# Linear attention into an MLP: joint tails, a reordered start, a held load and a split copy

## The chip, the cores and the metric

The program runs on one core of one Trainium2 chip. The metric is the device time of one execution in microseconds (us), taken as the median of several runs. The kernel before has a median of 296.78 us over 9 runs, from 296.37 to 297.11.

The engines are named as in the profile: PE is TensorE's matrix multiply and PEld its weight load, DVE is VectorE, ACT is ScalarE, POOL is GpSimd, and SP is SyncE, which only issues DMAs here. Every engine works through its own instructions in order.

## The reference

The inputs q, k and v have 8 batches, 8 heads, 576 positions and 64 features per head. Linear attention feeds an MLP (w_in is 512x2048, w_out is 2048x512, beta has 2048 entries):

```
phi(x) = where(x > 0, x, exp(x) - 1) + 1
kv  = sum over s of phi(k)[s, :, None] * v[s, None, :]      # per batch and head
z   = sum over s of phi(k)[s]
x   = (phi(q) @ kv) / (phi(q) @ z + 1e-6)                   # heads side by side: 4608 x 512
h   = x @ w_in
out = (h * sigmoid(beta * h)) @ w_out                       # float32, 4608 x 512
```

The kernel computes in bf16 with f32 accumulation. The loads of q, k, v and w_in cast from f32 to bf16 on the way, w_out is divided by beta on the chip, and the gate is then one Silu with a scale of beta.

## The kernel before, in words

**Tiles.** A batch has 576 rows: four tiles of 128 (t = 0 to 3) and a tail of 64 (t = 4, `NJ`). The MLP runs on the four full tiles of one batch at a time (512 columns), and once more, as batch `B` = 8, on the tails of all batches, which are gathered in `xT_tail` (8 x 64 columns). Batch 0 is laid out in another way: nine rows j on 64 partitions, with two groups of four heads on the lower and the upper half of the partitions (`nine`, `load_nine`, and the functions that end in 0).

**Stages of a batch n.** Exp on ScalarE (`exp_`), max(x, 0) + 1 on DVE (`relu`) and their minimum (`phi`, which gives phi of the reference). `v_copy` puts v beside a column of ones. `kv_mm` makes kv and z on TensorE: 40 small matmuls, alternating between output rows 0-63 and 64-127. `kv_evac` copies them out of PSUM into the block-diagonal `kv_bd[n % 2]`. phi(q) is transposed on TensorE (`q_trans`, batches 0 and 1) or by one DMA issued from SP (`q_trans_dma`, from batch 2). Then for each tile: `num_mm` (four matmuls of 130 columns), `num_norm` (three DVE instructions: add, reciprocal, multiply) and the transpose of the result into `xT`, by TensorE (`x_trans`, batches 0 to 2, with a copy out of PSUM) or by a DMA from SP (from batch 3, `DMA_T`).

**MLP.** `h_phase` does h for the 16 blocks of 128 of d_ff, each four matmuls and one Silu on ScalarE. `y_phase` (or `y_phase_wide`, four tiles side by side, for batches 0 and 1) multiplies by w_out; each tile of y is copied and stored by SP.

**Order.** It is written out by hand (`manual_schedule`). While batch b is in its MLP, batch n = b + 1 is prepared: a `plan` gives, for an index i, the functions that are issued after group i of an h_phase, or after ff block i (and then after tile i - 12) of `y_phase_wide`, or after every four ff blocks in `y_phase`. From batch 2 on this is one loop (for b in 2 to 8). A function's instructions enter the in-order queues of their engines at that place.

**Buffers.** PSUM: four banks in the pool `mm`, and two double banks in the pool `att`, used in turn by kv_mm, num_mm, the "wide" transposes and the last h blocks of batches 0 and 1. `xqk` has three buffers, `vraw` and `vaug` two each, `q_pT` two.

**Loads.** GpSimd issues the casting loads, in order: batch 0's k, q (j < 4), v (j < 6), v (rest), q (rest), the four pieces of w_in, w_out's first two pieces, batch 1's k and q, and so on. `load_next(b)` issues six DMAs (main part and tail of k, q and v). `load_next(3)` is issued in y_phase_wide(0), `load_next(4)` in h_phase(1), and later ones after an h_phase.

**The start.** To occupy TensorE before data arrive, `warm` multiplies a zeroed tile. Batch 0 then goes through exp0, relu0, phi0, kv_mm0, q_trans0 and num_mm for tiles 0 and 1; the second part of q (j from 4) is worked on between.

**Lines.** Large matmuls are L453 (h) and L505 (y); num_mm is L399, x_trans L433, kv_mm L344, kv_evac L355, q_trans L380, copies out of PSUM L372 (ACT) and L370 (DVE), v_copy L370, exp L229, Silu L445, num_norm L413 to L415, batch 0's loads L131, other loads L72 and L76, w_in L159, silu_table L581, warm L575.

Of the kernel before, what the change touches and what calls it, by code (L numbers as in the profile page):

```python
# [16 lines left out]
def kernel(  # L17
# [99 lines left out]
    def nine(a, spec):  # L117

        names = " ".join(spec)
        flat = a.rearrange("p a b c -> p (a b c)")  # L120
        size = {"h": HH, "j": N9, "d": D}
        n = size["h"] * size["j"] * size["d"]
        return flat[:, 0:n].rearrange(f"p ({names}) -> p {names}", **size)

    q9 = nine(xqk[0][:, 0], "hjd")
    k9 = nine(xqk[0][:, 1], "hjd")
    v9 = nine(vraw[0], "hjd")

    def load_nine(dst, src, h0=0, h1=HH, j0=0, j1=N9):
        for g in range(2):  # L130
            nc.gpsimd.dma_start(  # L131
                out=dst[g * TAIL : (g + 1) * TAIL, h0:h1, j0:j1, :].rearrange(
                    "p h j d -> p h (j d)"
                ),
                in_=src[0, g * HH + h0 : g * HH + h1, :, :]
# [7 lines left out]
    nc.vector.memset(g_sb[0][:, FC - 1, :], 0.0)  # L143
    clear_tail(1)
    nc.vector.memset(vraw[1][TAIL:P, :, NJ, :], 0.0)
    beta_row = consts.tile([FC, P], F32)
    nc.sync.dma_start(out=beta_row, in_=moe_beta.rearrange("(c p) -> c p", p=P))
# [3 lines left out]
    load_nine(k9, k)  # L151
    load_nine(q9, q, j1=4)
    make_identity(nc, identity)
    make_identity(nc, ident16)
    load_nine(v9, v, j1=6)
    load_nine(v9, v, j0=6)
    load_nine(q9, q, j0=4)
# [90 lines left out]
    x0 = {0: q9, 1: k9}  # L248
# [4 lines left out]
    def exp0(a, j0, j1):  # L253
        if j0 == 0:
            st["e0", a] = work9("e", bufs=3)
        nc.scalar.activation(  # L256
            st["e0", a][:, j0:j1].rearrange("p j h d -> p h j d"), x0[a][:, :, j0:j1],
            ACTF.Exp,
        )

    def relu0(a, j0, j1):
        if j0 == 0:
            st["r0", a] = work9("r")
        nc.vector.tensor_scalar(
            st["r0", a][:, j0:j1].rearrange("p j h d -> p h j d"), x0[a][:, :, j0:j1],
# [3 lines left out]
    def phi0(a, j0, j1):  # L269
        nc.vector.tensor_tensor(  # L270
            st["p0"][a][:, j0:j1], st["r0", a][:, j0:j1], st["e0", a][:, j0:j1], ALU.min
        )

    def q_trans0(t, banks, c0):


        for jj in range(2 if t < NJ else 1):
            for a in range(2):
                for g in range(2):
# [4 lines left out]
                        st["p0"][0][gs, 2 * t + jj, 2 * a : 2 * a + 2, :],  # L284
# [4 lines left out]
    def q_out0(t, banks, c0, dve):  # L289
        n = rows(t)  # L290
        src = banks[:, :, c0 : c0 + 2 * P].rearrange("p g (a n) -> p g a n", a=2)
        dst = st[0, "qT"][:, t].rearrange("p (g a) n -> p g a n", g=2)
# [483 lines left out]
```

## Time and profile before

| What | Value |
|---|---|
| median of 9 runs | 296.78 us |
| profiled execution, its own time | 297.11 us |
| its span, first to last instruction | 295.3 us |
| mean granted TensorE clock | 0.993 |
| first h matmul | 17.26 us |
| w_in's first piece, issued / landed | 8.39 / 17.2 us |
| first y matmul on record, batch 0 | 35.17 us |
| first h matmul of batches 1, 2, 3 | 52.82, 85.53, 116.66 us |
| HBM read, written | 36.71 MB, 9.44 MB |

Times are counted from the span's start. A timeline line gives start, duration, engine, line, operation, tiles (out<-in), shape, count, and in brackets the idle time of the engine before it with what ended that wait. "128*64" in a matmul is rows times columns of the weights, "128x130" the moving data. A matmul's duration runs to the end of its pipeline; the distance between starts is what it costs in a stream. A few matmul records are missing from a trace. A "stretch" line gives start:end and length, then each engine's busy time with its instructions, then the granted clock as a share of full speed, the DMA engines' mean busy share, and GB/s, which counts the bytes as written (bf16 where a load casts).

### The profile page before, as it was taken

How to read it: one execution, taken by the hardware profiler on the slowest of the kernel's cores; microseconds unless marked ns; L12 is line 12 of the kernel's file. 1: busy time of each engine (PE TensorE's matmuls, PEld its weight loads, DVE VectorE, ACT ScalarE, POOL GpSimd, SP SyncE). 2: the span in 40 equal slices, each digit the busy share in tenths (PEclk: the TensorE clock that was granted, in tenths of full speed). 3: DMA queues.
4: the chain of work that ended last, by engine and by line, in shares of the span. 5: the costliest groups of instructions: out<-in, count | busy, mean ns of one | idle time of the engine just before them, and what ended most of it. 6: DMA issues, size and time to landing. Idle time of an engine off the chain costs nothing.

```text
span 295.3 us, 4750 instructions
## 1 busy us (share of the span) xinstructions
PE 284.4 (96%) x1891; PEld 145.1 (49%) x1912; DVE 123.5 (42%) x261; ACT 175.3 (59%) x234; POOL 53.4 (18%) x72
## 2 busy tenths in 40 slices
PE   8879999999989999999999999999999999999994
PEld 3467446744555454445444544454445444444444
DVE  5665388504366164616461647154715400110012
ACT  2788795889988780778087907790770077018500
POOL 8924575540003200330023000000000000000000
PEclk9979999999999999999999999999999999999999
DMA  7999999999437993699369955024502400120032
GB/s 106 197 204 343 261 274 190 258 191 189 82 142 97 175 137 110 128 174 153 100 130 158 156 112 124 2 71 115 127 0 72 118 36 0 38 87 19 0 73 71
DMA packets 72310, 37.09 MB, mean 126 GB/s; under 512 B 40912, under 2 KB 66784, under 8 KB 72288
## 3 DMA queue, kind: packets, MB, share of 16 engines
q0 software_dynamic: 38912, 20.45, 47.7%
q1 hardware_dynamic: 33216, 16.20, 22.9%
q8 instruction: 15, 0.25, 0.3%
q10 hardware_dynamic: 160, 0.13, 0.2%
q14 instruction: 7, 0.06, 0.1%
HBM read 36.71 MB, written 9.44 MB: 156 GB/s over the span
## 4 chain that ended last, share of the span: by engine, by line
PE 80%; DMA 11%; ACT 3%; POOL 2%; issue 2%; DVE 0%; POOLq 0%
PE mm L453 37%; PE mm L505 35%; DMA xqk<-in_q_dram 5%; DMA vraw<-in_v_dram 3%; DMA w_in<-in_moe_w_in_dram 3%; PE att L399 3%; PE att L344 2%; POOL xqk L131 1%; PE mm L537 1%; PE att L453 1%; POOL vraw L131 1%; ACT e L229 1%; ACT g L445 1%; PE mm L433 1%; ACT L229 0%
## 5 line engine op out<-in xcount | busy, mean ns | idle before, releaser
L445 ACT ACTIVATE g<-mm,beta_c 128x512 bf16<-128x512 f32 (+2 forms) x156 | 97.3, 633 | 88.8 <-PE mm L453 88.6
L505 PE MATMUL mm<-w_out,g 128*128 128x512 bf16 x541 | 126.7, 379 | 1.2 <-issue 0.3
L453 PE MATMUL mm<-xT,w_in 128*128 128x512 bf16 (+2 forms) x560 | 108.9, 351 | 1.1 <-DMA w_in<-in_moe_w_in_dram 1.1
L453 PEld LDWEIGHTS <-w_in 128*128 128x128 bf16 x656 | 62.5, 99 | 62.1 <-DMA w_in<-in_moe_w_in_dram 1.2
L505 PEld LDWEIGHTS <-g 128*128 128x128 bf16 x560 | 52.9, 98 | 58.3
L515 DVE COPY y_sb<-mm 128x512 f32<-128x512 f32 x27 | 18.7, 691 | 70.6 <-PE mm L505 69.1
L229 ACT ACTIVATE e<-xqk 128x2560 bf16<-128x2560 bf16 x14 | 31.9, 2329 | 0.1
L415 DVE TENSOR_TENSOR xs<-att,rden 128x512 bf16<-128x512 f32 (+1 forms) x40 | 27.6, 690 | 1.4
L242 DVE TENSOR_TENSOR qk_p<-r,e 128x2560 bf16<-128x2560 bf16 x14 | 20.9, 1492 | 13.2 <-ACT e L229 12.4
L72 POOL DMA_DIRECT2D vraw<-in_v_dram x7 | 7.0, 996 | 85.0 <-DVE vaug L370 79.0
L355 DVE CAST kv_bd<-att 64x130 bf16<-64x130 f32 x28 | 8.2, 292 | 32.7 <-PE att L344 32.3
L413 DVE TENSOR_SCALAR den<-att 128x8 f32<-128x8 f32 (+1 forms) x40 | 6.5, 161 | 32.9 <-PE att L399 32.8
L399 PEld LDWEIGHTS <-q_pT 128*128 128x128 bf16 (+1 forms) x160 | 12.0, 102 | 10.1 <-DVE xs L415 2.4
L399 PE MATMUL att<-kv_bd,q_pT 128*128 128x130 bf16 (+1 forms) x160 | 16.2, 226 | 0.7 <-DVE kv_bd L370 0.7
L453 PE MATMUL mm<-xT_tail,w_in 128*128 128x512 bf16 x63 | 13.9, 379 | 0.1
L237 DVE TENSOR_SCALAR r<-xqk 128x2560 bf16<-128x2560 bf16 x14 | 11.4, 817 | 3.9 <-DMA xqk<-in_q_dram 2.4
L575 PE MATMUL mm<-g 128*128 128x512 bf16 x34 | 9.4, 435 | 1.2 <-DVE g L143 1.2
L229 ACT ACT_TABLE_LOAD x7 | 9.0, 1283 | 0.1
L414 DVE RECIPROCAL rden<-den 128x8 f32<-128x8 f32 (+1 forms) x40 | 8.1, 202 | 1.4
L72 POOL DMA_DIRECT2D xqk<-in_k_dram x7 | 6.8, 977 | 5.8 <-DMA w_in<-in_moe_w_in_dram 2.8
L76 POOL DMA_DIRECT2D xqk<-in_k_dram x7 | 7.4, 1062 | 1.6 <-DMA w_in<-in_moe_w_in_dram 1.6
L256 ACT ACTIVATE e<-xqk 128x1280 bf16<-128x1280 bf16 (+1 forms) x4 | 4.4, 1155 | 5.5 <-DMA xqk<-in_k_dram 4.9
(71 smaller groups left out, 140.4 us busy)
## 6 DMA issues: line engine op xcount, KB each, us to landing
out_dram<-y_sb SPq DMA_DIRECT2D x28, 256.0 KB, 2.3
xqk<-in_k_dram POOLq DMA_DIRECT2D x7, 512.0 KB, 10.6
xqk<-in_q_dram POOLq DMA_DIRECT2D x7, 512.0 KB, 11.6
vraw<-in_v_dram POOLq DMA_DIRECT2D x7, 512.0 KB, 11.2
w_in<-in_moe_w_in_dram POOLq DMA_DIRECT2D x4, 512.0 KB, 11.5
g<-in_moe_w_out_dram POOLq DMA_DIRECT2D x4, 512.0 KB, 10.7
out_dram<-y_sb SPq DMA_DIRECT2D x14, 128.0 KB, 5.2
xqk<-in_moe_w_out_dram POOLq DMA_DIRECT2D x2, 512.0 KB, 14.6
```

The lines of the kernel that those rows point to most:

```text
L72: eng.dma_start(out=dst[:, :, 0:NJ, :].rearrange("p h j d -> p h (j d)"), in_=src[b, :, 0:MAIN, :].rearrange("h (p j) d -> p h (j d)", j=NJ),)
L229: nc.scalar.activation(st[b, "e", a][:, h0:h1], xqk[b % NX][:, a, h0:h1], ACTF.Exp)
L237: nc.vector.tensor_scalar(st[b, "r", a][:, h0:h1], xqk[b % NX][:, a, h0:h1], 0.0, 1.0, ALU.max, ALU.add)
L242: nc.vector.tensor_tensor(st[b, "p"][:, a].rearrange("p j (h d) -> p h j d", h=H)[:, h0:h1], st[b, "r", a][:, h0:h1], st[b, "e", a][:, h0: ...
L355: nc.vector.tensor_copy(kv_bd[b % 2][i][gs, :, g, :], st[b, "kvp"][gs, 2 * i : 2 * i + 2, :])
L399: nc.tensor.matmul(nps[:n, p // 2, c0 : c0 + 2 * (D + 1)], st[b, "qT"][:, t, p, :n], kv_bd[b % 2][p // 2][:, p % 2], start=True, stop=True ...
L415: nc.vector.tensor_mul(xs[:n], nv[:, :, :, 0:D], rden[:n, :, :, None].to_broadcast([n, 2, 4, D]))
L445: nc.scalar.activation(g_sb[b % 2][:, ff, c0:c1], hp[:, c0:c1], ACTF.Silu, scale=beta_c[:, ff : ff + 1],)
L453: nc.tensor.matmul(hp[:, c0:c1], w_in_sb[ff // 4][:, kc, (ff % 4) * P : (ff % 4 + 1) * P], x[:, t0:t1, kc, :] if b < B else x[:, kc, c0:c1 ...
L505: nc.tensor.matmul(yp, g_sb[b % 2][:, ff, t * P : (t + 1) * P], w_out_sb[ff // 4][:, ff % 4, :], start=(ff == 0), stop=(ff == FC - 1),)
L515: nc.vector.tensor_copy(y_sb, yp)
L575: nc.tensor.matmul(st["warm"], g_sb[0][:, FC - 1, 0:P], g_sb[0][:, FC - 1, :], start=True, stop=True, skip_group_check=True,)
```

## The change

**Joint tails.** The tails of batches b - 1 and b (b = 1, 3, 5, 7) are normalized together. num_mm(b, NJ) does eight matmuls, batch b - 1 into rows 0-63 and batch b into rows 64-127; num_norm works on 128 rows, and one DMA transpose from SP puts the result into 128 columns of xT_tail, for all batches. The even batches' tail steps and the x_trans of tails go.

**Start.** The last four of batch 0's nine k rows per partition (`KF` = 5) are loaded as f32 by SP into `k_last`, a part of g_sb[1], instead of by GpSimd with a cast; exp and relu read it there. beta's load is issued by ScalarE. v is split at 5 instead of 6. There are 25 warm matmuls instead of 30; make_beta comes after the phi steps; kv_mm0 is interleaved with the arrival of v, the second q tile is transposed after kv's copies, and num_norm(0, 0) is issued ahead of exp and relu of q's second part. Tiles 2 to 4 of q are transposed together (`q_rest`), and copied by both engines.

**Batch 1.** v_copy(1) is done half by DVE, half by ScalarE; kv_mm(1) moves from index 9 to index 10 of y_phase_wide(0), directly ahead of the q transposes.

**Batch 2.** DVE instead of ScalarE copies the x_trans results, and x_trans(2, 1) moves from index 13 to 14.

**Held load.** load_next(4) moves from h_phase(1) to h_phase(2), index 8, behind a one-element copy on GpSimd that reads the last element of batch 3's transposed q.

Functions that ended in 0 now end in 9; these renamings are left out below.

```diff
+    x9 = [nine(xqk[0][:, a], "hjd") for a in range(2)]
     v9 = nine(vraw[0], "hjd")
+    QF = 4
+    KF = 5
+    k_last = g_f[:, 0 : HH * (N9 - KF) * D].rearrange(
+        "p (h j d) -> p h j d", h=HH, j=N9 - KF
+    )
...
+    load_nine(k_last, k, KF, N9, eng=nc.sync)
     clear_tail(1)
...
-    nc.sync.dma_start(out=beta_row, in_=moe_beta.rearrange("(c p) -> c p", p=P))
+    nc.scalar.dma_start(out=beta_row, in_=moe_beta.rearrange("(c p) -> c p", p=P))
...
-    load_nine(k9, k)
-    load_nine(q9, q, j1=4)
+    load_nine(x9[1][:, :, 0:KF], k, 0, KF)
+    load_nine(x9[0][:, :, 0:QF], q, 0, QF)
...
-    load_nine(v9, v, j1=6)
-    load_nine(v9, v, j0=6)
-    load_nine(q9, q, j0=4)
+    load_nine(v9[:, :, 0:KF], v, 0, KF)
+    load_nine(v9[:, :, KF:N9], v, KF, N9)
+    load_nine(x9[0][:, :, QF:N9], q, QF, N9)
...
     def num_mm(b, t):
...
-            nc.tensor.matmul(
-                nps[:n, p // 2, c0 : c0 + 2 * (D + 1)],
-                st[b, "qT"][:, t, p, :n],
-                kv_bd[b % 2][p // 2][:, p % 2],
-                start=True, stop=True, skip_group_check=True,
-            )
+            for i in range(1 if t < NJ else 2):
+                bb, n, r0 = (b, P, 0) if t < NJ else (b - 1 + i, TAIL, i * TAIL)
+                nc.tensor.matmul(
+                    nps[r0 : r0 + n, p // 2, c0 : c0 + 2 * (D + 1)],
+                    st[bb, "qT"][:, t, p, :n],
+                    kv_bd[bb % 2][p // 2][:, p % 2],
+                    start=True, stop=True, skip_group_check=True,
+                )
...
-        if by_dma(b):
+        if by_dma(b) or t == NJ:
             nc.sync.dma_start_transpose(
...
-        return xT_tail[:, :, b * TAIL : (b + 1) * TAIL]
+        return xT_tail[:, :, (b - 1) * TAIL : (b + 1) * TAIL]
...
+    held = consts.tile([1, 1], BF16)
+
+    def held_load(b, n):
+        nc.gpsimd.tensor_copy(held, st[n, "qT"][0:1, NJ, KC - 1, 0:1])
+        load_next(b)
...
     warm(10)
     beta_trans()
+    warm(15)
+    exp9(1, 0, KF)
+    exp9(1, KF, N9)
+    exp9(0, 0, 2)
+    exp9(0, 2, QF)
+    relu9(1, 0, KF)
+    relu9(1, KF, N9)
+    phi9(1, 0, KF)
+    relu9(0, 0, QF)
+    phi9(1, KF, N9)
+    phi9(0, 0, 2)
+    phi9(0, 2, QF)
     make_beta()
-    warm(20)
...
-    kv_mm0(kvp, 0, N9, False)
+    kv_mm0(kvp, 0, KF, False)
+    kv_mm0(kvp, 0, KF, True)
+    kv_mm0(kvp, KF, N9, False)
     qb = att_banks(BF16)
-    q_trans0(0, qb, 0)
-    q_trans0(1, qb, 256)
-    q_out0(0, qb, 0, False)
-    q_out0(1, qb, 256, False)
-    kv_mm0(kvp, 0, 6, True)
-    kv_mm0(kvp, 6, N9, True)
-    kv_evac0(kvp)
+    q_trans9(0, qb, 0)
+    q_out9(0, 1, qb, 0, False)
+    kv_mm0(kvp, KF, N9, True)
+    kv_evac9(kvp)
+    q_trans9(1, qb, 256)
+    q_out9(1, 2, qb, 256, False)
...
     num_mm(0, 1)
-    exp0(0, 4, N9)
-    relu0(0, 4, N9)
+    num_norm(0, 0)
+    exp9(0, QF, N9)
+    relu9(0, QF, N9)
     silu_table()
-    num_norm(0, 0)
-    phi0(0, 4, 6)
     warm(4)
     x_trans(0, 0, dve=True)
+    num_norm(0, 1)
+    phi9(0, QF, 6)
+    phi9(0, 6, N9)
...
-            3: [F(x_trans, 0, 1), F(num_mm, 0, 2), F(num_norm, 0, 2), F(q_rest0)],
-            5: [F(num_mm, 0, 3), F(num_norm, 0, 3)],
-            7: [F(x_trans, 0, 2)],
-            8: [F(num_mm, 0, 4), F(num_norm, 0, 4)],
-            9: [F(x_trans, 0, 3), F(tidy0)],
-            12: [F(x_trans, 0, 4)],
+            1: [F(x_trans, 0, 1)],
+            3: [F(q_rest)],
+            5: [F(num_mm, 0, 2), F(num_norm, 0, 2)],
+            7: [F(num_mm, 0, 3), F(num_norm, 0, 3)],
+            8: [F(x_trans, 0, 2)],
+            10: [F(x_trans, 0, 3, dve=True), F(tidy)],
...
-    v_copy(1)
+    v_copy(1, 0, HH)
+    v_copy(1, HH, H, dve=False)
     phi(1, 0)
     y_phase_wide(0, {
         4: [F(load_next, 3)],
-        9: [F(kv_mm, 1), F(kv_evac, 1), F(w_out_scale, 3)],
-        10: [F(q_trans, 1, 0, 1, wide=True), F(q_trans, 1, 2, 3, wide=True)],
+        10: [
+            F(kv_mm, 1), F(kv_evac, 1), F(w_out_scale, 3),
+            F(q_trans, 1, 0, 1, wide=True), F(q_trans, 1, 2, 3, wide=True),
+        ],
...
-            3: [F(x_trans, 1, 4)],
...
-            12: [F(v_copy, 2), F(load_next, 4)],
+            12: [F(v_copy, 2)],
...
-        12: [F(num_mm, 2, 1), F(num_norm, 2, 1), F(x_trans, 2, 0, wide=True)],
-        13: [F(num_mm, 2, 2), F(num_norm, 2, 2), F(x_trans, 2, 1, wide=True)],
-        14: [F(num_mm, 2, 3), F(num_norm, 2, 3)],
+        12: [F(num_mm, 2, 1), F(num_norm, 2, 1), F(x_trans, 2, 0, wide=True, dve=True)],
+        13: [F(num_mm, 2, 2), F(num_norm, 2, 2)],
+        14: [
+            F(x_trans, 2, 1, wide=True, dve=True), F(num_mm, 2, 3), F(num_norm, 2, 3),
+        ],
...
-                0: [F(x_trans, 2, 2), F(num_mm, 2, 4), F(num_norm, 2, 4)],
-                1: [F(x_trans, 2, 3)],
-                3: [F(x_trans, 2, 4)],
+                0: [F(x_trans, 2, 2, dve=True)],
+                1: [F(x_trans, 2, 3, dve=True)],
...
+            if b == 2:
+                plan[4 + o] = [F(held_load, 4, n)]
...
-            for t in range(NT):
+            for t in range(NT if n % 2 else NJ):
```

## The prediction

> **What bounds the kernel now.** I read the busy times and the slices first, then the chain of waits, then the stretches of the start, then the timeline wherever TensorE's stream of large matmuls is broken.
>
> ```profile
> PE 284.4 (96%) x1891; PEld 145.1 (49%) x1912; DVE 123.5 (42%) x261; ACT 175.3 (59%) x234; POOL 53.4 (18%) x72
> PE   8879999999989999999999999999999999999994
> PEclk9979999999999999999999999999999999999999
> ```
>
> TensorE is busy for 96%, so time can be gained only by taking work out of its stream, closing a gap, or starting it earlier. A 128x512 matmul starts every 0.216 us (24 y matmuls at 111.47: 5.35 us less the last one's 0.38, over 23). The h and y matmuls at that pace are 18 x 64 x 0.216 = 249 us; the other 46 are start, attention and waits. The chain of waits says the same: TensorE, except at the beginning.
>
> Three stretches of the start, and two on either side of 18.12 (columns: length; busy time of PE, PEld, DVE, ACT, POOL; granted clock; DMA share; GB/s):
>
> ```profile
> 1.50:2.50 1.00, 1.00 (x4) 0.32 (x3) 0.89 (x4) 0.73 (x2) 1.00 (x2) 1.00 0.03 8
> 2.50:3.20 0.70, 0.70 (x3) 0.29 (x2) 0.69 (x3) 0.00 (x0) 0.70 (x3) 1.00 0.56 35
> 3.20:13.70 10.50, 9.14 (x124) 5.00 (x124) 5.36 (x19) 4.76 (x7) 9.87 (x19) 1.00 1.29 188
> 14.71:18.12 3.41, 1.49 (x28) 1.26 (x29) 2.95 (x8) 2.83 (x6) 0.65 (x2) 1.00 1.24 206
> 18.12:21.53 3.41, 3.41 (x42) 2.97 (x40) 1.36 (x5) 2.69 (x8) 0.97 (x2) 0.50 1.24 207
> ```
>
> The DMA engines are nearly empty until 3.2 although GpSimd issued at 1.25, and full from then on. After 3.41 us with 1.49 us of matmul the clock is at half for 3.41 us.
>
> The breaks that the change touches, from the timeline (start, duration, instruction, idle time and who ended it):
>
> ```profile
> 17.26 0.73 PE L453 MATMUL mm<-xT,w_in 128*128 128x128 bf16 x10 [1.07 <-DMA w_in<-in_moe_w_in_dram]
> ...
> 24.45 0.60 PE L453 MATMUL mm<-xT,w_in 128*128 128x256 bf16 x4
> 24.98 0.29 PE L433 MATMUL mm<-identity,xs 64*128 64x64 bf16 x4
> 25.20 0.28 PE L453 MATMUL mm<-xT,w_in 128*128 128x256 bf16 x1
> ...
> 43.83 0.20 ACT L581 ACTIVATE small<-small 128x1 f32<-128x1 f32 x1
> 43.90 0.82 PE L344 MATMUL att<-vaug,qk_p 128*64 128x65 bf16 x40
> 44.76 1.21 DVE L355 CAST kv_bd<-att 64x130 bf16<-64x130 f32 x4 [0.54 <-PE att L344]
> 45.53 1.12 PE L380 MATMUL att<-identity,qk_p 128*128 128x128 bf16 x16
> ...
> 80.97 1.03 PE L505 MATMUL mm<-w_out,g 128*128 128x512 bf16 x4
> 83.35 0.38 PE L433 MATMUL att<-identity,xs 128*128 128x128 bf16 x4 [1.12 <-ACT xT L372]
> 83.57 1.03 PE L505 MATMUL mm<-w_out,g 128*128 128x512 bf16 x3
> ...
> 140.02 1.03 PE L505 MATMUL mm<-w_out,g 128*128 128x512 bf16 x4
> 140.98 0.42 PE L399 MATMUL att<-kv_bd,q_pT 128*64 128x130 bf16 x4
> 141.33 0.39 PE L505 MATMUL mm<-w_out,g 128*128 128x512 bf16 x1
> ```
>
> **Part 1, the tails.** A piece of attention work costs TensorE what it delays the next large matmul beyond its pace. A 64-row tail's num_mm: 141.33 - 140.02 - 4 x 0.216 = 0.45. A full tile's is 0.23 (109.30 after eight matmuls from 107.34). A tail's x_trans: 25.20 - 24.45 - 4 x 0.109 = 0.31. The change takes out three x_trans (b = 0, 1, 2) and makes eight num_mm four, with eight matmuls each, alternating output rows 0-63 and 64-127. The nearest row with that alternation is kv_mm: 40 matmuls of 65 columns in 0.82 us, which one after another need 40 x 65/512 x 0.216 = 1.10 us. So the halves run beside each other, and I take 0.45 for a joint tail; bounds 0.25 and 0.67 (the second four in a row, 0.22 more). Gain: 4 x 0.45 + 3 x 0.31 = 2.7, of which b = 0 brings 0.76. DVE does four norms (1.2 us each) fewer. SP sends four tail transposes instead of five; none is needed before xT_tail's own h_phase.
>
> **Part 2, batch 0's start.** The first h matmul waited 1.07 us for w_in. Now SP issues 4/9 of batch 0's k (0.52 MB read, 0.26 MB as the 188 GB/s are counted, 1.4 us of that stream) in the time when the DMA engines are empty. beta_row, issued by SP at 0.75, landed at 2.28, so SP's data can flow from about 1.5, 1.7 us before the stream is full. I take 1.2 us off every landing that follows, bounds 0 (both queues share the engines, none gains) and 1.7. The Trainium skill, in "DMA: Bandwidth & Descriptors", section "Issuing engines are not separate DMA queues", speaks against it: issuing from another engine saves only sequencer time, since all queues end on the same 16 engines. By it w_in[0] stays at 17.2 and the sum is 1.2 higher, at 294.0; the trace's empty 1.7 us are why I don't follow it.
>
> The computing ahead of h gets shorter too. num_norm(0, 0) no longer waits for q's second part and its relu (0.62 + 0.58 us on DVE ahead of 14.38), and xT[0] should be ready at about 14.5, against w_in[0] at 16.0: 1.5 us of cover, free. Under it lie: relu on f32 (between 0.44 for bf16 and 2 x 0.48 for w_out's f32 rows), make_beta (1.1 us, now while DVE waits for kv_mm0), exp in one piece more (0.2), the last q transposes, and beta_row from ScalarE (issue 0.41, landing 1.5, after the table load at 2.2: about 4.2, read at 5.08). If the cover goes, each costs itself. SP has nothing queued behind its two issues until the first store at 49.
>
> The clock: five warm matmuls fewer, and a gap of 1.5 us before h. I count some 2.1 us of matmul in the 3.41 us where 1.49 led to half clock; the stretch 11.30 to 14.71 had 2.70 and did not. Full clock would save 1.0 (batch 0's insertions and waits add up to 3.9 us, and need 2.2 plus the tails' 0.76). Midway, so half: 0.5; bounds 0 and 1.0. The Trainium skill, in "TensorE: Matmul & The Clock Gate", section "What's actually happening", has it that an idle window of about 3.4 us halves the clock; by that rule a stretch with 2.1 us of work keeps it full, and the sum is 0.5 lower, 292.3, but here 1.49 us did not.
>
> **Part 3, batch 1's attention in y_phase_wide(0).** This costs. ScalarE is free at 44.03 and then copies half of v (1.27, the row of 1280 columns), until 45.30. kv_mm waits for that. The y matmuls start at 34.95; one step later in the plan than before TensorE arrives at 34.95 + 44 x 0.216 = 44.5: 0.85 of waiting with the weight load. The second pair of q transposes takes kv_mm's PSUM banks (two in turn), free after kv_evac, 1.25 us after kv_mm. Until now four y matmuls hid most of that; now only the first pair does (0.45): 0.8 bare. Together 1.65, against 0.25 for the same places now: +1.4; bounds 0 (if v lands late enough to hide the copy anyway) and 1.9. Behind the copy on ScalarE are the q_pT copies, which wait for TensorE anyhow. DVE saves 0.3 on its half.
>
> **Part 4, batch 2.** The x_trans at 83.35 waited 1.12 us for ScalarE, busy with exps and table load until 82.1, to empty a bank. From 81.83 to 83.57 lie 1.74 us, of which 0.23 + 0.22 are work: 1.29 of loss. With DVE copying, the bank is free at 82.2; next is num_mm(2, 3), waiting for num_norm(2, 2) on DVE until 83.4, 0.3 after TensorE gets there. Gain 1.0, bounds 0.6 and 1.3.
>
> **Part 5, the held loads.** GpSimd waits for batch 3's q transpose (landed 96.29; without loads beside it 4.8 us instead of 6.1, so about 95 on this clock), then issues six loads of batch 4 and, queued behind, six of batch 5. At the cadence of 93.46 to 106.69 (6.6 us to the first landing, 3.1 for each next), k lands at 102 and q at 105; ScalarE's exps may end as late as 116. No wait in front of TensorE, cost 0; batch 2's q transpose gets faster than its 8.3, which it needs only by 0.3. Bounds 0 and +1.0 (the x transposes of batch 3, below).
>
> **Sum.** -1.2 (start) -0.5 (clock) -2.7 (tails) +1.4 (batch 1) -1.0 (batch 2) + 0 = -4.0. The profiled execution was 297.11 with a span of 295.3 and 1.8 around it; it is 0.33 above the median of 296.78, and I take the difference from the median: 292.8.
>
> **Rivals.**
> - *The early issue brings nothing* (SP's part delays GpSimd's equally), and the clock falls again. For: the engines are full from 3.2 on. Against: the empty 1.7 us. 292.8 + 1.7 = 294.5.
> - *The joint tail's halves run one after another.* For: no row shows 130 columns so. Against: kv_mm. 4 x 0.22 more: 293.7.
> - *Slower: batch 3's x transposes sink under the held loads.* Loads now fill 92 to 114, with the x transposes among them. The last (111.22, landed 2.4 later) has 3.0 until h_phase(3) at 116.66. For: batch 2's q transpose took 8.3 beside loads against 4.8 without. Against: that ratio gives 4.2, within the slack. Each us beyond it costs one, and 4.0 of stall undo the gain: 2.4 + 3.0 + 4.0 = 9.4 us for one transpose; at 11 the time is 298.4.
>
> **How the numbers follow.** Forecast 0.50 (its own range 291.2 to 294.0), first rival 0.22, second 0.10, third 0.10, and 0.08 for gaps of the start that I don't see, half of them slower. A measurement of this kernel can't tell less than 0.2% (0.6 us) from no change. Faster: 0.50 + 0.22 + 0.10 + 0.01. Slower: most of the third, the half of the last, and a part of what could go wrong at once: 0.13; the rest is the same. The range: down to 291.0 (the clock restored, the batch 1 cost at half), up to 296.0 (first rival with batch 1 at its upper bound and 1.0 of part 5).
>
> **What would show it.** w_in[0] landing near 16.0, the first h matmul there; the granted clock after 18; no 64-row x_trans before the end; joint num_mm rows with 0.45 of delay; kv_mm(1) ending an idle stretch that ScalarE's vaug copy releases; no ACT xT wait near 80; batch 4's k landing before ScalarE asks. Wrong: if the first h matmul starts at 17 or later, or a wait on an xT transpose stands ahead of h_phase(3).

## The result, and the profile after

The changed kernel takes 299.49 us (median of 10 runs, 298.79 to 300.99) against 296.47 for the kernel before (32 runs). The ratio is 1.0109, 95% interval 1.0095 to 1.0122: slower by 3.0 us, where 4.0 us faster was forecast. The profiled execution took 299.45 with a span of 297.7.

The page of the changed kernel: busy times, TensorE's slices, its granted clock.

```profile
PE 284.1 (95%) x1875; PEld 143.4 (48%) x1895; DVE 122.1 (41%) x257; ACT 172.3 (58%) x226; POOL 50.8 (17%) x73
...
PE   8889998999999994999999999999999999999994
...
PEclk9899999999999999899999999999999999999999
```

TensorE's 16th slice (111.6 to 119.1 us) has a 4 where the kernel before had a 9, and the clock's 17th has an 8. The chain of waits names the work it stood still for (start, duration, what; "issue" is time in which the engine waited for nothing that the profile shows).

```profile
106.87 0.65 PE mm L529 x3
107.52 0.05 issue
107.57 0.92 PE mm L529 x4
108.49 9.67 DMA xT<-xs
118.16 0.14 issue
118.29 6.78 PE mm L477 x23
```

The 9.67 us are the last x transpose of batch 3, from its issue by SyncE at 108.49 to its landing; in the kernel before it took 2.4 (111.22 to 113.65). The first group of h_phase(3) reads it. It is the fourth in SyncE's queue: the four were issued at 102.20, 104.58, 106.11 and 108.49 and landed at 109.30, 112.23, 115.33 and 118.16, the first after 7.10 and each further one about 3 behind the one ahead of it. The views of the tile xT from 98 to 125 us, the kernel before first (durations of the issuing in ns, first and last issue; then the time from issue to landing), and TensorE at this place in the kernel before:

```profile
L419 SPq DMA_TRANSPOSE xT<-xs x4: 1189/1205/1814, 104.8 to 111.2; - x4
...
DMA to landing us min/median/max: 2.4/2.8/3.9
```
```profile
L443 SPq DMA_TRANSPOSE xT<-xs x4: 1193/1262/1528, 102.2 to 108.5; - x4
...
DMA to landing us min/median/max: 7.1/8.4/9.7
```
```profile
111.47 5.35 PE L505 MATMUL mm<-w_out,g 128*128 128x512 bf16 x24
116.66 1.67 PE L453 MATMUL mm<-xT,w_in 128*128 128x512 bf16 x7
```

Two stretches of the changed kernel around this place, and two from its start (columns: length; busy time of PE, PEld, DVE, ACT, POOL; granted clock; DMA share; GB/s):

```profile
9.03:12.44 3.41, 2.51 (x90) 1.95 (x90) 3.27 (x10) 2.62 (x6) 3.41 (x6) 1.00 1.38 196
12.44:15.86 3.42, 3.03 (x15) 1.65 (x16) 2.10 (x7) 3.35 (x5) 1.82 (x3) 0.50 1.24 208
114.85:118.26 3.41, 0.00 (x0) 0.00 (x0) 3.29 (x5) 0.00 (x0) 0.00 (x0) 1.00 1.42 197
118.26:121.67 3.41, 3.38 (x9) 1.21 (x10) 2.08 (x2) 0.69 (x1) 1.04 (x2) 0.50 1.27 262
```

3.41 us without a matmul are followed by 3.41 us at half clock. So the wait is paid twice. And the timeline of the changed kernel at the breaks that the prediction showed for the kernel before (start, duration, instruction, idle time and who ended it):

```profile
16.84 0.62 PE L477 MATMUL mm<-xT,w_in 128*128 128x128 bf16 x8 [0.69 <-DMA w_in<-in_moe_w_in_dram]
...
43.11 0.99 PE L365 MATMUL att<-vaug,qk_p 128*64 128x65 bf16 x40
...
44.13 1.21 DVE L376 CAST kv_bd<-att 64x130 bf16<-64x130 f32 x4 [0.66 <-PE att L365]
...
45.40 0.62 PE L401 MATMUL att<-identity,qk_p 128*128 128x128 bf16 x8 [0.75 <-DVE kv_bd L376]
...
82.10 0.39 PE L457 MATMUL att<-identity,xs 128*128 128x128 bf16 x4
...
106.71 1.89 PE L529 MATMUL mm<-w_out,g 128*128 128x512 bf16 x7
108.53 0.42 PE L423 MATMUL att<-kv_bd,q_pT 128*64 128x130 bf16 x8
108.88 5.35 PE L529 MATMUL mm<-w_out,g 128*128 128x512 bf16 x24
118.29 1.01 PE L477 MATMUL mm<-xT,w_in 128*128 128x512 bf16 x2 [4.06 <-DMA xT<-xs]
```

Three things are as meant: the joint tail at 108.53 (eight matmuls) delays the next large matmul by 108.88 - 106.71 - 8 x 0.216 = 0.44; the x transpose of batch 2 at 82.10 has no ScalarE wait in front; no 64-row x_trans is left before the end. The second pair of q transposes at 45.40 waits 0.75 for kv_bd. The last line is the damage.

Where the time went, by the first matmul of each phase and the last of all (us in each profiled execution; three experiments are in the table because the text comes back to them):

| | before | after | x1_no_hold | x2_hold_only | x5_hold_q2 |
|---|---|---|---|---|---|
| h_phase(0) | 17.26 | 16.84 | 15.67 | 17.55 | 16.97 |
| y_phase_wide(0) | 35.17 | 33.52 | 32.53 | 34.53 | 33.23 |
| h_phase(1) | 52.82 | 52.19 | 51.62 | 52.18 | 52.02 |
| y_phase_wide(1) | 67.90 | 67.06 | 66.49 | 67.26 | 66.89 |
| h_phase(2) | 85.53 | 83.72 | 89.53 | 84.89 | 83.56 |
| y_phase(2) | 101.47 | 98.88 | 104.69 | 100.83 | 98.72 |
| h_phase(3) | 116.66 | 118.29 | 119.88 | 121.00 | 113.91 |
| y_phase(3) | 131.33 | 134.62 | 134.55 | 138.57 | 128.58 |
| h_phase(4) | 146.52 | 149.35 | 149.29 | 153.76 | 143.31 |
| last matmul's end | 291.56 | 293.95 | 293.88 | 298.80 | 287.91 |

Up to y_phase(2) the changed kernel is ahead by 2.59. Between y_phase(2) and h_phase(3) it loses 4.22 (19.41 instead of 15.19), in h_phase(3) 1.66 more (16.33 instead of 14.67), and later it wins 0.90: -2.59 + 4.22 + 1.66 - 0.90 = +2.39. By the medians it is 3.0: the profiled execution of the kernel before is 0.64 above its median (297.11 against 296.47), with a half clock from 18.12 that most of its executions don't have (below, "The clock at the start").

### The profile page after: what moved, and what is told of

It is laid out like the page before. It is cut to its first block, busy times and chain, and to the rows that moved or that the text cites. A ratio compares the mean times of both kernels' runs of the same rounds, so it can differ in the third digit from the quotient of the medians.

```text
span 297.7 us, 4708 instructions
## 1 busy us (share of the span) xinstructions
PE 284.1 (95%) x1875; PEld 143.4 (48%) x1895; DVE 122.1 (41%) x257; ACT 172.3 (58%) x226; POOL 50.8 (17%) x73
## 4 chain that ended last, share of the span: by engine, by line
PE 88%; DMA 5%; DVE 3%; issue 2%; POOL 0%; DVEq 0%; POOLq 0%
PE mm L477 40%; PE mm L529 38%; DMA xT<-xs 3%; PE att L423 3%; PE att L477 2%; PE att L365 2%; DMA xqk<-in_k_dram 2%; PE mm L561 1%; DVE xs L439 1%; PE mm L457 1%; PE mm L606 0%; DVE kv_bd L376 0%; PE att L457 0%; DVE qk_p L283 0%; DVE rden L438 0%
## 5 line engine op out<-in xcount | busy, mean ns | idle before, releaser
L439 DVE TENSOR_TENSOR xs<-att,rden 128x512 bf16<-128x512 f32 x36 | 24.9, 691 | 1.5 <-DVE rden L438 0.2
L437 DVE TENSOR_SCALAR den<-att 128x8 f32<-128x8 f32 x36 | 5.9, 163 | 27.6 <-PE att L423 27.4
L423 PEld LDWEIGHTS <-q_pT 128*128 128x128 bf16 (+1 forms) x160 | 11.0, 102 | 9.0 <-DVE xs L439 1.9
L423 PE MATMUL att<-kv_bd,q_pT 128*128 128x130 bf16 (+1 forms) x160 | 14.5, 226 | 0.3 <-DVE kv_bd L391 0.2
L438 DVE RECIPROCAL rden<-den 128x8 f32<-128x8 f32 x36 | 7.3, 203 | 1.2
L72 POOL DMA_DIRECT2D xqk<-in_k_dram x7 | 6.8, 974 | 5.2 <-DMA w_in<-in_moe_w_in_dram 2.8
L477 PE MATMUL att<-xT,w_in 128*128 128x512 bf16 x32 | 7.2, 379 | 0.0
```

Of the source, the lines that this page charges most:

```text
L72: eng.dma_start(out=dst[:, :, 0:NJ, :].rearrange("p h j d -> p h (j d)"), in_=src[b, :, 0:MAIN, :].rearrange("h (p j) d -> p h (j d)", j=NJ),)
L423: nc.tensor.matmul(nps[r0 : r0 + n, p // 2, c0 : c0 + 2 * (D + 1)], st[bb, "qT"][:, t, p, :n], kv_bd[bb % 2][p // 2][:, p % 2], start=True ...
L439: nc.vector.tensor_mul(xs[:n], nv[:, :, :, 0:D], rden[:n, :, :, None].to_broadcast([n, 2, 4, D]))
L477: nc.tensor.matmul(hp[:, c0:c1], w_in_sb[ff // 4][:, kc, (ff % 4) * P : (ff % 4 + 1) * P], x[:, t0:t1, kc, :] if b < B else x[:, kc, c0:c1 ...
```

## The experiments

Each is a change of one of the two kernels, timed beside the kernel before. The theory to be tested: the whole loss comes from the place of batch 4's loads, which GpSimd holds until batch 3's q is transposed, and the rest of the change brings what it should.

**x1_no_hold: the change without the hold.**

```diff
-            12: [F(v_copy, 2)],
+            12: [F(v_copy, 2), F(load_next, 4)],
...
-            if b == 2:
-                plan[4 + o] = [F(held_load, 4, n)]
```

> The change without its held load: batch 4's load is issued in h_phase(1) as in the kernel before, all else as changed. Theory (the held loads of batch 4, with batch 5's behind them, fill the stretch in which batch 3's x tiles are transposed, and TensorE waits 4.1 us for the last tile, then runs 3.4 us at half clock): both go, 5.9 us, so about 293.5 us, ratio to the kernel before 0.988 to 0.991, and h_phase(3) starts without a wait on xT. Rival (the x transposes are slow because of the other parts, such as the joint tails' wider transposes in SP's queue): still 299, with the last x transpose over 7 us.

Measured: 298.11 (295.35 to 299.40), ratio 1.0047 (1.0023 to 1.0070). A miss: the kernel without the hold is still slower than before. The profiled execution, 299.40, is the slowest of the twelve, so the wait below is the longest case. The timeline of x1_no_hold and its view of the tile q_pT between 60 and 90 us:

```profile
81.88 0.61 PE L423 MATMUL att<-kv_bd,q_pT 128*128 128x130 bf16 x4 [4.01 <-DMA q_pT<-qk_p]
```
```profile
L409 SPq DMA_TRANSPOSE q_pT<-qk_p x1: 6861/6861/6861, 69.2 to 69.2; - x1
...
DMA to landing us min/median/max: 12.7/12.7/12.7
```

The wait at h_phase(3) is gone, but a wait of the same length stands at batch 2's first num_mm. Batch 4's loads now run where they ran in the kernel before, and batch 2's q transpose (issued at 69.16) is beside them: 12.7 us. In the kernel before it was issued at 70.59, took 8.3, and landed at 78.86, 0.26 before TensorE needed it. Here its request comes 1.4 earlier, and so does TensorE, but it lands at 81.84, 3.0 later: batch 4's v, the last of the three loads (in two pieces), lands at 78.04 and 79.33 instead of 74.53 and 75.10. About half of these 3.5 to 4.2 us goes with the new DMA transpose of the joint tail of batches 0 and 1 (issued at 54.02, landed at 62.09), which lies among these loads: batch 3's v takes 14.8 from issue to landing in the two traces without this transpose (before, x2_hold_only) and 16.4 to 16.8 in five with it (x1, x5, x8, x12 and the changed kernel). Where the rest comes from wasn't tried. Behind the wait the clock is at half for 6.83 us (80.23 to 87.06), and y_phase_wide(1) takes 23.04 instead of 16.66 in the changed kernel. So the other parts of the change had used up a margin of 0.26 us and made the transpose later besides, and the hold isn't an ornament: it takes the loads away from batch 2's q transpose and puts them on batch 3's x transposes.

**x2_hold_only: the kernel before, with the held load alone.**

```diff
-            12: [F(v_copy, 2), F(load_next, 4)],
+            12: [F(v_copy, 2)],
...
+            if b == 2:
+                plan[4 + o] = [F(held_load, 4, n)]
```

> The kernel before with the held load alone. Theory: batch 3's x transposes take 6 to 10 us instead of 2.4 here too, a wait of 3 to 5 us ahead of h_phase(3) and half clock after it: 300 to 303 us, ratio 1.015 to 1.02. Rival (the hold hurts only together with the joint tails or the earlier PE): within 0.5 us of the kernel before.

Measured: 304.05, ratio 1.0257 (1.0244 to 1.0271): 7.6 us for the hold alone. The direction is the theory's, the size is above its range. The tile xT from 98 to 125 us in x2_hold_only:

```profile
L419 SPq DMA_TRANSPOSE xT<-xs x4: 1252/1273/2298, 104.1 to 110.4; - x4
...
DMA to landing us min/median/max: 9.1/9.5/10.5
```

In the kernel before this was 2.4/2.8/3.9, in the changed one 7.1/8.4/9.7. The table gives the rest: 20.17 instead of 15.19 between y_phase(2) and h_phase(3), then 17.57 instead of 14.67 in h_phase(3), where the clock was at half for 6.83 us (120.08 to 126.90): 5.0 in front of h_phase(3) and 2.9 of clock.

**x4_warm_wait: the change, with TensorE kept busy through the wait.** This separates the wait from the half clock behind it.

```diff
         y_phase(b, plan)
+        if b == 2:
+            st["warm"] = mm_bank([P, 512])
+            warm(18)
```

> The changed kernel with 18 matmuls that nobody reads ahead of h_phase(3), 3.9 us at full clock, in the time in which TensorE waits for xT. They take nothing out of the wait. Theory (of the 5.9 us lost there, 4.1 are the wait and 1.7 the half clock after it): the start of h_phase(3) stays near 118.3 and the clock stays full after it, 1.5 to 1.8 us less than the changed kernel, about 297.8 us. Rival (the half clock costs nothing by itself, since DMA paces the stretch): same as the changed kernel within 0.5 us.

Measured: 297.28, ratio 1.0028 (1.0014 to 1.0042), 2.2 below the changed kernel. Timeline and stretches of x4_warm_wait:

```profile
113.56 4.05 PE L606 MATMUL mm<-g 128*128 128x512 bf16 x18
117.63 1.67 PE L477 MATMUL mm<-xT,w_in 128*128 128x512 bf16 x7
```
```profile
117.60:121.00 3.40, 3.37 (x17) 1.59 (x17) 2.22 (x2) 1.95 (x3) 0.88 (x2) 1.00 1.27 263
```

At their pace the y matmuls are through at 113.56, and h_phase(3) begins 4.07 later (4.2 in the changed kernel), just behind the last transpose's landing at 117.50, so the wait stays. But the clock behind it is full, and h_phase(3) takes 14.67 (117.63 to 132.30) instead of 16.33. The half clock is worth 1.66, shown by itself; most of the other 0.5 lies ahead of y_phase(2) (98.36 against 98.88), which this edit doesn't touch.

**x3_hold_both: batch 5's loads held as well,** until the last full x tile of batch 3 has landed.

```diff
-        load_next(b + 3)
+        if b != 2:
+            load_next(b + 3)
...
         y_phase(b, plan)
+        if b == 2:
+            nc.gpsimd.tensor_copy(held, xT[0][0:1, NJ - 1, KC - 1, 0:1])
+            load_next(5)
```

> The changed kernel with batch 4's load held as it is, and batch 5's load held too, until batch 3's last x tile has been transposed. Theory in its narrow form (it is the twelve loads in a row that reach over the x transposes; batch 4's alone are over by 106): the last x transpose, issued near 108.5, takes under 4 us, no wait, 293.0 to 294.0 us. Rival (batch 4's six loads alone are enough to delay the first transposes, and SP's queue then carries the delay to the last one): a wait of 1 to 3 us stays, 295 to 298 us.

Measured: 295.30, ratio 0.9970 (0.9954 to 0.9985). With only batch 4's loads (k, q and v) ahead, the x transposes of batch 3 land after 2.5 to 4.5 and h_phase(3) has no wait. But the loads of batch 5 have moved on to the next transposes. The timeline of x3_hold_both:

```profile
131.41 0.41 PE L423 MATMUL att<-kv_bd,q_pT 128*128 128x130 bf16 x4 [1.04 <-DMA q_pT<-qk_p]
...
145.18 2.10 PE L477 MATMUL mm<-xT,w_in 128*128 128x512 bf16 x9 [0.58 <-DMA xT<-xs]
```

Batch 4's q transpose took 14.2 (117.13 to 131.37) and y_phase(3) is 1.97 longer than in x5_hold_q2 (16.70 against 14.73), where that transpose took 4.9. So the transposes of either batch pay where loads are queued.

**x5_hold_q2: the hold one batch earlier,** until batch 2's q is transposed.

```diff
         1: [F(phi, 2, 0), F(q_trans_dma, 2), F(phi, 2, 1)],
+        2: [F(held_load, 4, 2)],
...
-            if b == 2:
-                plan[4 + o] = [F(held_load, 4, n)]
```

> The changed kernel, but batch 4's loads are held until batch 2's q is transposed (about 74.5 us in the changed kernel's trace) instead of batch 3's (92.9). Theory: the whole slowdown is the place of these loads. Released at 74.5 they take some 13 us on their queue and are over by about 90, so they lie after q's DMA transpose of batch 2 and before the x transposes of batch 3; only q's transpose of batch 3, issued near 88, may still touch their end. Then there is no wait in front of the first group of h_phase(3) and no half clock behind it: 299.5 - 4.2 - 1.7 = 293.6, between 292.5 and 294.5. Rival: transposes collide with whatever is loading, and the stall only moves once more, to q's transpose of batch 3 or to batch 4's; then 295 to 297.

Measured: 293.26 (293.18 to 293.42), ratio 0.9888 (0.9874 to 0.9903): faster than both kernels, 3.4 below the one before. The page of x5_hold_q2, its timeline at the old place of the wait, and its tile xT from 98 to 117 us:

```profile
PE   8879998999999999999999999999999999999994
...
PEclk9999999999999999999999999999999999999999
```
```profile
108.36 0.42 PE L423 MATMUL att<-kv_bd,q_pT 128*64 128x130 bf16 x8
108.72 5.35 PE L529 MATMUL mm<-w_out,g 128*128 128x512 bf16 x24
113.91 2.32 PE L477 MATMUL mm<-xT,w_in 128*128 128x512 bf16 x10
```
```profile
L443 SPq DMA_TRANSPOSE xT<-xs x4: 1188/1190/1191, 102.0 to 108.3; - x4
...
DMA to landing us min/median/max: 2.4/3.1/3.9
```

The 24 y matmuls run into h_phase(3) without a gap and the clock stays full. Batch 2's q transpose takes 4.9 (69.57 to 74.43), batch 4's loads run from 74.72 to 91.28, and batch 3's q transpose (87.90) meets only their end. This settles the cause: the same work, with the same loads released 18 us earlier, is 6.2 us faster (293.26 against 299.49).

The next seven runs ask how much each other part brings once the hold does no harm. Two build up to x5_hold_q2 from the kernel before, the others start from it. x9 to x12 ran on another chip than x1 to x8; the kernel before took 296.55 there, and 296.62 beside x5 to x8.

**x8_tails_hold_q2 and x12_tails_batch2.** x8 is the kernel before with the joint tails and the hold of x5_hold_q2; x12 adds the part for batch 2. The edits are those of the change, and for x12:

```diff
-        12: [F(num_mm, 2, 1), F(num_norm, 2, 1), F(x_trans, 2, 0, wide=True)],
-        13: [F(num_mm, 2, 2), F(num_norm, 2, 2), F(x_trans, 2, 1, wide=True)],
-        14: [F(num_mm, 2, 3), F(num_norm, 2, 3)],
+        12: [F(num_mm, 2, 1), F(num_norm, 2, 1), F(x_trans, 2, 0, wide=True, dve=True)],
+        13: [F(num_mm, 2, 2), F(num_norm, 2, 2)],
+        14: [
+            F(x_trans, 2, 1, wide=True, dve=True), F(num_mm, 2, 3), F(num_norm, 2, 3),
+        ],
```

> The kernel before with two parts of the change alone: the joint tails (even batches' tails with the next batch's), and batch 4's loads held, but until batch 2's q is transposed. If the tails are worth what the prediction gave them (2.7 us) and the hold at this place is free, this is 293.7 us against 296.4 for the kernel before, ratio 0.991. Rival: the hold at this place costs as well and the ratio is 1 or above.

> x8_tails_hold_q2 (the kernel before, with joint tails and batch 4's loads held until batch 2's q is transposed) and the change's part for batch 2: VectorE evacuates its x transposes, the second one a step later. What it still lacks of x5_hold_q2 is the new start and the v copy by two engines. The trace of x8_tails_hold_q2 loses 1.3 us to x5_hold_q2 at batch 2 and 0.1 elsewhere: 293.9, from 295.21. If the start and batch 1's part are worth nothing, it comes within 0.3 us of x5_hold_q2; if they are worth what the prediction gave (1.7 - 1.4 and less), it is 0.3 to 0.7 above it.

Measured: x8 295.21, ratio 0.9957 (0.9944 to 0.9970), 1.4 below before and not 2.7; x12 293.93, ratio 0.9910 (0.9897 to 0.9924), 0.67 above x5_hold_q2 (the two intervals overlap slightly). The timeline of x8_tails_hold_q2:

```profile
82.44 0.38 PE L436 MATMUL att<-identity,xs 128*128 128x128 bf16 x4 [1.12 <-ACT xT L372]
...
87.17 2.56 PE L456 MATMUL mm<-xT,w_in 128*128 128x256 bf16 x19 [0.19 <-ACT xT L372]
```

Both waits for ScalarE are gone in x12, and its trace is 1.23 shorter (289.33 to 288.10 at the last matmul): that is what batch 2's part is worth, 1.28 by the medians. For the tails, x8's trace against the one before: batch 0's tail really leaves the start (y_phase_wide(0) begins 16.26 behind h_phase(0), against 16.98 in x2_hold_only, which has the same start with the tails in it), but then y_phase_wide(0) takes 19.02 instead of 17.65. From h_phase(1) to the end x8 gains 1.53, near the 1.6 that the remaining tails add up to (0.31 + 0.77 + 2 x 0.44, less the second wait for ScalarE at 87.17, which puts that matmul 0.36 behind its pace).

**x6_batch1_undone and x9_phi_first: what sets y_phase_wide(0)?** The chain of waits of x5_hold_q2 there:

```profile
30.05 11.58 DMA vraw<-in_v_dram
...
41.72 0.06 DVE vaug L391
41.78 0.80 issue
42.58 1.47 DVE qk_p L245
44.05 0.20 DVE kv_bd L376
...
45.23 0.62 PE att L401 x8
```

Batch 1's v lands at 41.63, then VectorE copies, finishes phi of q, and casts kv_bd; only then does the second pair of q transposes go. v landed at 41.91 in the kernel before: it gains 0.3 where y_phase_wide(0) begins 1.9 earlier. x6 takes batch 1's part back out of x5_hold_q2, and x9 puts phi of q ahead of the copy and spreads the transposes:

```diff
-    v_copy(1, 0, HH)
-    v_copy(1, HH, H, dve=False)
+    v_copy(1)
...
-        10: [
-            F(kv_mm, 1), F(kv_evac, 1), F(w_out_scale, 3),
-            F(q_trans, 1, 0, 1, wide=True), F(q_trans, 1, 2, 3, wide=True),
-        ],
+        9: [F(kv_mm, 1), F(kv_evac, 1), F(w_out_scale, 3)],
+        10: [F(q_trans, 1, 0, 1, wide=True), F(q_trans, 1, 2, 3, wide=True)],
```
```diff
     phi(1, 1)
+    phi(1, 0)
     v_copy(1, 0, HH)
     v_copy(1, HH, H, dve=False)
-    phi(1, 0)
...
-            F(kv_mm, 1), F(kv_evac, 1), F(w_out_scale, 3),
-            F(q_trans, 1, 0, 1, wide=True), F(q_trans, 1, 2, 3, wide=True),
-        ],
-        11: [F(num_mm, 1, 0), F(num_norm, 1, 0)],
+            F(q_trans, 1, 0, 1, wide=True), F(kv_mm, 1), F(kv_evac, 1),
+            F(w_out_scale, 3),
+        ],
+        11: [
+            F(q_trans, 1, 2, 3, wide=True), F(num_mm, 1, 0), F(num_norm, 1, 0),
+        ],
```

> As x5_hold_q2, but v of batch 1 is copied whole by VectorE and kv_mm(1) goes back to the ninth place of y_phase_wide(0), the q transposes at the tenth. If the delay of 1.0 us that y_phase_wide(0) gained in the changed kernel is the price of this part, this is 0.7 to 1.0 us faster than x5_hold_q2. Rival: v's arrival and the whole copy put kv_mm as late as before, and the time is that of x5_hold_q2 within 0.3 us.

> x5_hold_q2 (the changed kernel with batch 4's loads held until batch 2's q is transposed), and in batch 1's part of y_phase_wide(0) VectorE's phi of q goes ahead of the copy of v, the first two q transposes ahead of kv_mm, the other two behind the next group. In x5_hold_q2 TensorE's q transposes stand behind VectorE's chain of v's landing (41.63), half copy, phi of q (1.47) and four kv_bd casts (1.2); the delay there is 2.96 us for 1.74 us of kv and transpose work. Theory: that chain is the bound of y_phase_wide(0), and the new order takes up to 1.2 us of waiting away: 292.0 to 292.6 against 293.26. Rival: v's landing alone is the bound, and the time stays within 0.3 us of x5_hold_q2.

Measured: x6 293.72, ratio 0.9904 (0.9891 to 0.9917); x9 293.56, ratio 0.9900 (0.9885 to 0.9916). Both expected gains failed. In x6's trace y_phase_wide(0) takes 18.77, in x5_hold_q2's 18.79: the part for batch 1 is worth nothing there either way (the 0.46 by which x6 is slower is in its trace before any edited line, where w_in[0] landed 0.44 later). In x9 the waits at the transposes do go, and come back two steps on; its timeline:

```profile
45.47 0.41 PE L423 MATMUL att<-kv_bd,q_pT 128*128 128x130 bf16 x4
...
48.33 0.40 PE L457 MATMUL att<-identity,xs 128*128 128x128 bf16 x4 [0.56 <-DVE xs L439]
```

TensorE reaches the x transpose earlier, and VectorE hasn't got its xs: y_phase_wide(0) takes 19.12. Taking this wait away doesn't shorten the stage; VectorE's next result is then late.

**x10_idle_h0 and x11_idle_h1: does the wait for v take up what is lost or won ahead of it?** Five more matmuls, read by nobody, in h_phase(0) or in h_phase(1).

```diff
             17: [F(w_out_scale, 0), F(w_out_scale, 1)],
+            20: [F(warm_more, 5)],
```
```diff
             12: [F(v_copy, 2)],
+            5: [F(warm_more, 5)],
```

> x5_hold_q2 with five more matmuls of 512 columns (1.07 us at full clock), read by nobody, in h_phase(0) behind its 21st group. Theory: what TensorE gains or loses ahead of y_phase_wide(0) is mostly taken up by the wait for batch 1's v, which the loads' queue sets (41.63 in x5_hold_q2, 41.91 in the kernel before); x5_hold_q2 has 1.2 us of waiting there, so the time grows by 0 to 0.4 us. Rival: the start's work sets the end one for one, and it grows by 1.07.

> x5_hold_q2 with the same five unread matmuls (1.07 us) in h_phase(1) instead, behind the wait for v. Theory: nothing behind that place waits for a load, so the time grows by 1.0 to 1.1 us. Rival: a later wait, such as for batch 2's q transpose, takes it up as well, and it grows by less than 0.5.

Measured: x10 294.49, ratio 0.9927 (0.9910 to 0.9944), +1.2; x11 294.57, ratio 0.9936 (0.9916 to 0.9956), +1.3. In h_phase(1) the theory held, one for one: that phase takes 1.08 longer in the trace (15.95 against 14.87). The median is 0.2 above that, but four of its six executions have a mean clock of 0.992 to 0.994, which none of x5_hold_q2's four has. In h_phase(0) the theory failed by the medians: the added 1.07 wasn't taken up (two of the six executions have a clock of 0.992; the other four are 0.4 to 1.4 above x5_hold_q2). Its trace shows how little is: y_phase_wide(0) began at 33.73 instead of 33.23 (0.50 later; h_phase(0) had begun 0.87 earlier, without any edit there), and h_phase(1) 0.39 later, so 0.11 of 0.50 was absorbed.

With the changed order y_phase_wide(0) takes 18.66 to 18.79 wherever it begins between 33.0 and 34.7 (after, x3, x4, x5, x7, x10, x11), and 19.09 only at 32.53 (x1). With the old order it takes 17.65 where it begins at 34.5 or later (before, x2), and 18.77 to 19.02 at 33.1 to 33.7 (x6, x8, x12). The waits of TensorE for the copy of v between 15 and 48 us, in x8 and in x6 (what waited for what: us, times, longest; in the kernel before there is none):

```profile
PE att L344 <- DVE vaug L370: 0.9, 1, 0.9
```
```profile
PE att L365 <- DVE vaug L391: 0.7, 1, 0.7
```

So the old order does wait for v when TensorE comes early, and the changed one has a cost of its own of 1.0, early or late; at the start as it is now, they come out alike.

**x7_k_by_gpsimd: who loads k's last parts.**

```diff
-    load_nine(k_last, k, KF, N9, eng=nc.sync)
...
     load_nine(x9[1][:, :, 0:KF], k, 0, KF)
+    load_nine(k_last, k, KF, N9)
```

> As x5_hold_q2, but the last four of k's nine parts are loaded by GpSimd behind its first five, instead of by SyncE. If SyncE's early issue is what brought the first matmul of h_phase(0) 0.42 us forward, this is 0.4 us slower than x5_hold_q2. Rival: w_in's arrival sets the start and doesn't depend on who loads k, no difference (within 0.2 us).

Measured: 294.95, ratio 0.9952 (0.9937 to 0.9967): 1.7 slower than x5_hold_q2, in the theory's direction but four times its size. The timeline of x7_k_by_gpsimd:

```profile
18.40 0.62 PE L477 MATMUL mm<-xT,w_in 128*128 128x128 bf16 x8 [1.63 <-DMA w_in<-in_moe_w_in_dram]
```

The first h matmul is 1.43 later than in x5_hold_q2 (16.97), and so is w_in[0]'s landing (18.36 against 16.93). GpSimd issues a load of this kind every 0.6 us, and now twelve instead of ten stand ahead of w_in: it is issued at 9.70 instead of 8.30. So SyncE's two issues pay for the split of k in two, which the change itself brought; the kernel before, with k whole, also had ten loads ahead of w_in, issued at 8.39. Against that kernel SyncE's two issues save no time on GpSimd.

## Why the prediction was wrong, step by step

**Part 5 is the step that failed.** "No wait in front of TensorE, cost 0", with bounds 0 and +1.0, became a loss of 4.22 in front of h_phase(3), 4.06 of it in one wait, and a half clock of 1.66 behind it. The mechanism was on the page as the third rival, with its place (the last x transpose of batch 3 ahead of h_phase(3)) and its price ("9.4 us for one transpose" undoes the gain); the transpose took 9.67. What failed is the estimate that spoke against it: "that ratio gives 4.2, within the slack". It took the ratio of batch 2's q transpose (8.3 beside loads, 4.8 without), where the loads ended at 75.10, 4.5 us behind the issue, and carried it to a place where six loads of batch 4 and six of batch 5 keep their queue full from 93 to 125 (the rival has them end at 114). And it priced one transpose, where four stand one behind the other in SyncE's queue. A ratio from a partly covered transpose says nothing about a wholly covered one. It had the right order of events and the wrong size. And the rival charged only the wait: that 3.4 us of idling halve the clock was told in Part 2, and not charged in Part 5.

**Part 1, the tails: right in the piece, short in the sum.** A joint tail costs 0.44 to 0.45 as taken, so the second rival is out. Of the 2.7, the 0.76 of batch 0 leaves the start (0.72 in the traces), but x8 then loses 1.37 in y_phase_wide(0); the rest is there.

**Part 2, the start: mis-sized.** Taken 1.2 off every landing. w_in[0], which the first h matmul waits for, came 0.42 earlier (17.21 to 16.79), and that is less than executions differ: with this same start it landed anywhere from 15.47 (x4) to 17.37 (x6). h_phase(0) begins at 15.67 to 17.41 in the nine traces with this start, on average at 16.66, and at 16.84 to 17.55 in the four with the old one (before, x2, x8, x12), on average at 17.16: 0.5, not 1.2. The landings of w_in[1] to w_in[3] came 1.0 earlier than in the profile before (19.71, 22.27, 24.83 became 18.71, 21.22, 23.78), but with the old start they came at 19.07, 21.66, 24.19 in x8 and at 18.84, 21.44, 23.97 in x12, so that the early issue brought this isn't shown. What it did is to fill the DMA engines sooner: 35 and 202 GB/s in the stretches 1.50:2.50 and 2.50:3.20 instead of 8 and 35 (SyncE's part counted as f32). Also "xT[0] should be ready at about 14.5" was off: the copy ended at 16.61 (half clock) in the changed kernel and at 15.61 in x1_no_hold, so the cover was no 1.5 us. The Trainium skill's sentence in "DMA: Bandwidth & Descriptors", section "Issuing engines are not separate DMA queues", that issuing from another engine saves only sequencer time, came nearer than my 1.2, and x7_k_by_gpsimd agrees with it: with the two issues back on GpSimd, w_in[0] is issued 1.40 later and lands 1.43 later.

**The clock at the start.** The half clock moved from 18.12 to 12.44 and was not removed; the stretch ahead of it had 2.51 us of matmul, more than the 1.49 and the 2.1 I argued from. Among the other traces with the same start it comes in x4 and x11 (from 11.19 and 11.81) and not in x1, x3, x5, x6, x9 and x10. What decides it at the start stays open. Where it comes in the kernel before it costs 0.93, near the 1.0 taken: h_phase(0) takes 17.91 there and 16.98 in x2_hold_only, which is the same up to that place and has no half clock. But the forecast took its 0.5 off the median, and there was little of it in the median: of the 50 executions of the kernel before that were timed beside the experiments, 45 have a mean clock of 0.997 or more, where the profiled one has 0.993. At 118 the rule that the prediction cited from the Trainium skill ("TensorE: Matmul & The Clock Gate", section "What's actually happening", an idle window of about 3.4 us) agrees with the row: 3.41 us with no matmul, then half clock; at 12.44 it doesn't, behind 2.51 us of work.

**Part 3, batch 1: size nearly right, one cause wrong.** The y matmuls start at 35.17, not at 34.95, which is the row of their first weight load. kv_mm hardly waits for ScalarE's half copy (0.99 us for work of 0.82; 0.85 had been charged), because it begins on VectorE's half; the bare second pair costs 0.75 as said. The delay from kv_mm to the next large matmul goes from 1.82 (with four y matmuls between, one of them missing in the trace) to 3.06, and the whole of y_phase_wide(0) from 17.65 to 18.67: +1.02, against +1.4. That undoing it gains nothing (x6) I hadn't seen: once TensorE is 1.5 earlier, the old order waits for v and loses as much.

**Part 4, batch 2: right.** -1.0 forecast; y_phase_wide(1) takes 16.66 instead of 17.63, -0.97. Between x8 and x12 it is 1.23 by the traces, where 0.36 belong to the second wait for ScalarE that x8 alone has.

All parts but the fifth, in x5_hold_q2, give 293.26 against the 292.8 that were forecast for all. That is nearer than the parts are, and in part luck: the start brought some 0.7 less than was taken and the clock hardly any of its 0.5, while batch 1 cost 0.3 to 0.4 less.

## What to carry to other kernels

When loads are moved, ask which small transfers run at the new place, and price one such transfer under a queue that stays full, by a row where it is wholly covered; a ratio from a partly covered one is no bound. A release point just behind one transpose is also a point ahead of the next ones: count how long the released loads run (here 3.1 us for each k, q or v alone, and 6.3 beside the transposes: 112.57, 118.88, 125.23) and what is issued in that time. And a wait of 4 us in front of TensorE costs its length and a stretch of half clock behind it, here 1.7.

## What the runs showed that I had not expected

**A transpose behind queued loads doesn't begin, and then shares by packets.** Packets begun per us in the packet records of two traces, GpSimd's load queue beside SyncE's transposes and stores:

```
us from    changed kernel            kernel before
           loads   SyncE             loads   SyncE
104          549       0               406       0
105          599       0               565      12
106          282     143                47     532
107          234     235                 0     144
112          233     234                 0     544
```

In the changed kernel the transpose issued at 102.20 moves no packet until 106.26, 4.06 us later; in the kernel before, the one issued at 104.78 starts after 1.17. From 106 on the two queues alternate nearly one for one, but a packet of the loads has up to 512 bytes and one of the transposes 256: 120 KB against 60 between 107 and 108. No run was made for the late start, but the traces show what it goes with. In those of both kernels, x1, x2, x3 and x5, up to 150 us, a transpose with no other under way moves its first packet 1.17 to 1.61 us after its issue when at most two load DMAs are under way, after 2.14 and 2.60 with four, and after 4.05 to 4.28 with five or more (nine cases).

**GpSimd's loads go eight deep.** The nineteenth load of the kernel before is issued at 17.50, 0.29 behind the landing of the eleventh (w_in[0], 17.21); in x6_batch1_undone the tenth is issued at 8.67, 0.29 behind the second's at 8.38, and its lateness carries through to w_in. A load that lands late delays the issue of the one eight places behind it, and of all that follow. The profile shows GpSimd's issue waiting for that landing, so it is a wait of the program; how many loads the queue itself would take isn't shown.

**A margin of 0.26 us.** The kernel before stood that close to the wait that x1_no_hold ran into. There TensorE came 1.4 earlier and the transpose landed 3.0 later. A change that only brings TensorE forward by 1.4 would have cost about 1.1 there, if the landing stayed where it was (an estimate from these numbers).
